# Taking the low part of the attention output through PSUM: one subtraction moved from VectorE to TensorE and ScalarE

## The chip, the cores and the metric

The kernel runs on one core of one Trainium2 chip. A core has five engines with a queue of instructions each: TensorE (PE in the tables, its weight loads PEld), VectorE (DVE), ScalarE (ACT), GpSimd (POOL) and SyncE (SP), which here only issues DMAs. The metric is the time of one execution in microseconds (us) on the device. The profile comes from one profiled execution of the same program.

## The reference

What is computed is a chain of three layers over a batch of 8 sequences of 576 positions with 512 features: attention in chunks of 64, a gated layer whose gate is a convolution over 5 positions, and a normalised two-matrix layer with a residual. Cut to its core:

```python
scores = np.matmul(q_c, k_c.transpose(0, 1, 2, 4, 3)) / np.sqrt(D)   # 64 x 64 in each chunk and head
scores = scores - np.max(scores, axis=-1, keepdims=True)
attn = np.exp(scores)
attn = attn / (np.sum(attn, axis=-1, keepdims=True) + 1e-09)
x = np.matmul(attn, v_c)                       # then heads are laid side by side: 512 features

for k in range(5):
    gate_pre += conv_w[k] * xp[:, k:k + S, :]  # xp is x with 4 zeros in front
gate = 1.0 / (1.0 + np.exp(-gate_pre))
x = gate * (x @ w_val) @ w_out

xn = (x - mu) / np.sqrt(var + 1e-06) * g_ln
out = x + np.maximum(xn @ w_ch1, 0.0) @ w_ch2  # 512 -> 2048 -> 512
```

Everything is float32. The large products are made with float32r operands, and each operand is split in a high part (its copy in float32r) and a low part (what the copy left), and a product is three matmuls: high by high, low by high, high by low.

## The kernel before

The 4608 positions are cut into 18 units of 256 and 9 blocks of 512 (two units make a block). In the first part of the program one slot follows another, one per unit. A slot issues, in this order: the scores of a unit (`a3`, tile `sc`, softmax on VectorE with tiles `mx`, `ex`, `sm`, `pr`), the turned weights of the unit before (`a4`, PSUM tile `pst`, copied by ScalarE to `pT`), and its product with the values (`a5`, PSUM tile `x`, two banks, one buffer). Between these stand the pieces of the gated layer for earlier blocks: the convolution (`conv`: one ScalarE instruction and four VectorE instructions for each of four slices of `cg`), its sigmoid (`sigm`, one ScalarE instruction over `cg`), the product with `w_val` (`val`: four chains of 12 matmuls into PSUM tile `psv`; `gv` multiplies by the gate on VectorE, `gh` and `gl` are its two parts) and the product with `w_out` (`proj`: four chains into `pso`, copied to `y` and stored). The chains of `psv` and `pso` share a pool of two PSUM buffers, so the third chain of `val` starts when `gv` has read the first.

After `a5` three copies of `x` are made: `xf` in float32, which the convolution reads, `xh`, the high part, and `xl`, the low part, which `val` reads a slot later. ScalarE makes `xf` (L233) and `xh` (L236), VectorE makes `xl` from `x` and `xh` (L238). Where a sequence begins inside a unit, `xf` has a gap of four columns there, and all three are made in two pieces (`segs`).

Weights come as 64-bit words and are decoded to float32 by one ScalarE and three VectorE instructions for each 128x512 tile (`decode`, tile `da`, L87 to L90). In the first part this is done for `w_val`, `w_out` and, by `early_ff`, for the first four pairs of tiles of the two last matrices.

From some 303 us on the second part (`ff1`, `ff2`, then `ff_pair`) does the last layer, almost all of it matmuls.

PE's order is as written in the code for the first four slots and in the second part. In the rest of the first part, and on the other engines, a scheduler places the instructions ahead of time, by its own estimates and by priorities; on the chip each engine then works strictly through its list.

Of the kernel before, what the change touches and what calls it, by code (L numbers as in the profile page):

```python
# [9 lines left out]
F32R = mybir.dt.float32r  # L10
U32 = mybir.dt.uint32
ACTF = mybir.ActivationFunctionType
ALU = mybir.AluOpType
# [6 lines left out]
def tile_chunk_attention_gated_mlp(ctx: ExitStack, tc: tile.TileContext, qk, v, w_val, conv_w, w_out, g_ln, w1, w2, out):  # L20
    nc = tc.nc
# [9 lines left out]
    P = 128  # L31
    BLK = 512
    UN = 256
    UPB = BLK // UN
    NB = NT // BLK
    NU = NT // UN
# [4 lines left out]
    LAG = 1  # L41
# [3 lines left out]
    scale = 1.0 / float(D) ** 0.5  # L45
    outf = out.rearrange("b s d -> (b s) d")

    def boundary(j):
        o = (-(j * BLK)) % S
        return o if 0 < o < BLK else BLK  # L50

    const = ctx.enter_context(tc.tile_pool(name="const", bufs=1))
# [18 lines left out]
    ident = const.tile([P, P], F32, name="ident")  # L71
    cw = const.tile([P, (KC + 1) * CT], F32, name="cw")
    gr = const.tile([CT, P], F32, name="gr")


    qkr, vr = {}, {}

    def load_qkv(u):
        t = qkr[u] = pA.tile([P, 2, NP, UN], F32, tag="qk", name="qkr")
        nc.sync.dma_start(out=t.rearrange("p a h t -> p (a h t)"), in_=qk[u])  # L80
        t = vr[u] = pA.tile([P, NC, NP, D], F32, tag="vr", name="vr", bufs=3)
        nc.sync.dma_start(out=t.rearrange("p c h d -> p (c h d)"), in_=v[u])
# [18 lines left out]
    def load_w(w, nm, slot0):  # L101
        raws = []
        for c in range(CT):
            raw = wA.tile([P, DM, 2], U32, tag=f"s{slot0 + c}", name="raw")
            nc.sync.dma_start(out=raw, in_=w[c * P:(c + 1) * P])
            raws.append(raw)
        wv[nm] = raws
# [73 lines left out]
    def a4(u):  # L181
        pr = pt.pop(u)
        t = pA.tile([P, NG, P], F32, tag="pT", name="pT", bufs=1)
        ps = ps_p.tile([P, NG, P], F32, tag="p", name="pst")
        for g in range(NG):
            nc.tensor.transpose(out=ps[:, g, :], in_=pr[:, g].rearrange("p r k -> p (r k)"), identity=ident)
        with tc.high_priority():
            nc.scalar.activation(out=t, in_=ps, func=ACTF.Copy)
            pT[u] = t

    xf, xh, xl = {}, {}, {}

    def new_block(j):
        o = boundary(j)
        t = pD2.tile([P, CT, BLK + 2 * HALO], F32, tag="xf", name="xf")
        if j == 0:
            nc.gpsimd.memset(t[:, :, 0:HALO], 0.0)
        else:
            ob = boundary(j - 1)
            e = BLK + (HALO if ob < BLK else 0)  # L200
            nc.gpsimd.tensor_copy(out=t[:, :, 0:HALO], in_=xf[j - 1][:, :, e:e + HALO])
        if o < BLK:
            nc.gpsimd.memset(t[:, :, HALO + o:2 * HALO + o], 0.0)
        xf[j] = t
        xh[j] = pD2.tile([P, CT, BLK], F32R, tag="xh", name="xh")
        xl[j] = pD2.tile([P, CT, BLK], F32R, tag="xl", name="xl")

    def a5(u):
        t = pT.pop(u)
        j, uu = divmod(u, UPB)  # L210
        va = vr.pop(u)
        x = ps_x.tile([P, 2, NP // 2, UN], F32, tag="x", name="x")
        for i in range(NP // 2):
            for c in range(NC):
                n, cs = c // 2, slice(c % 2 * CH, (c % 2 + 1) * CH)
                for f in range(2):
                    for r in range(2):
                        r0, o0 = CH * r, CH * f
                        nc.tensor.matmul(
                            out=x[o0:o0 + CH, r, i, c * CH:(c + 1) * CH],  # L220
                            lhsT=va[r0:r0 + CH, c, 2 * i + f, :],
                            rhs=t[r0:r0 + CH, n * NP + 2 * i + f, cs],
                            start=True, stop=True,
                        )
        if uu == 0:
            new_block(j)
        o = boundary(j)
        a, b = uu * UN, (uu + 1) * UN
        segs = [(max(a, lo), min(b, hi), sh) for lo, hi, sh in ((0, o, HALO), (o, BLK, 2 * HALO)) if max(a, lo) < min(b, hi)]
        with tc.high_priority():  # L230
            for lo, hi, sh in segs:
                dst = xf[j][:, :, lo + sh:hi + sh].rearrange("p (r i) t -> p r i t", r=2)
                nc.scalar.activation(out=dst, in_=x[:, :, :, lo - a:hi - a], func=ACTF.Copy)  # L233
            for lo, hi, sh in segs:
                dst = xh[j][:, :, lo:hi].rearrange("p (r i) t -> p r i t", r=2)
                nc.scalar.activation(out=dst, in_=x[:, :, :, lo - a:hi - a], func=ACTF.Copy)  # L236
                low = xl[j][:, :, lo:hi].rearrange("p (r i) t -> p r i t", r=2)
                nc.vector.tensor_tensor(out=low, in0=x[:, :, :, lo - a:hi - a], in1=dst, op=ALU.subtract)  # L238


    cg = pD1.tile([P, CT, BLK + HALO], F32, name="cg")
# [334 lines left out]


    make_identity(nc, ident)
    load_qkv(0)
    load_w(w_val, "v", 0)  # L580
    load_qkv(1)
# [4 lines left out]
    def warm(u, i):  # L586

        n = WARM.get((u, i), 0)
        if n:
            ps = ps_d.tile([P, BLK], F32, tag="d", name="psw")  # L590
            for _ in range(n):
                nc.tensor.matmul(out=ps[:, 0:P], lhsT=ident, rhs=ident, start=True, stop=True)

    def slot(u):
        d = [dense.get((u, i), []) for i in range(4)]
        if u + 2 < NU:
            load_qkv(u + 2)
        warm(u, 0)
        if u < NU:
            a3(u)  # L600
        warm(u, 1)
        for fn in d[0]:
            fn()
        if LAG <= u < NU + LAG:
            a4(u - LAG)
        warm(u, 2)
        for fn in d[1]:
            fn()
        if LAG <= u < NU + LAG:
            a5(u - LAG)  # L610
        warm(u, 3)
        for fn in d[2] + d[3]:
            fn()

    dense = {}
# [45 lines left out]
    for j in range(NB):  # L661
        u = UPB * (j + 1) + LAG - 1
# [20 lines left out]
    for u in range(NU + LAG + 4):  # L683
        if u == MANUAL:
            head.close()
        slot(u)
        if u == NU + LAG - 1:
            with tc.high_priority():
                sigm(NB - 1)
            prep()  # L690
# [58 lines left out]
    for s in range(NS):  # L749
        for p in range(NPR):  # L750
# [5 lines left out]
            if s + 1 < NS and 2 <= p < 6:  # L756
                i = 2 * (p - 2)
# [43 lines left out]
```

## Time and profile before

| | |
|---|---|
| median of 3 runs | 1139.91 us (1138.92 to 1139.91) |
| span of the profiled execution, first to last instruction | 1134.2 us |
| median less that span | 5.7 us |
| busy in the span: PE, weight loads | 1070.5 us (94%), 871.4 us (77%) |
| busy in the span: DVE, ACT, POOL | 712.8 us (63%), 483.5 us (43%), 110.6 us (10%) |

The page gives the span of the profiled execution, and no time of its own around it; the 5.7 us between its span and the median of the runs are taken as what lies before and after the instructions. Shares of the whole span mix the two parts: in the second part PE works almost without a pause, in the first it doesn't. The ends of matmuls are modelled, and one ends after the next has begun, so the distance between starts says what a matmul takes.

### The profile page before, as it was taken

Reading aid. Unit: us, or ns where it says so; the run is one execution under the profiler, and the core shown is the slowest. Engines: PE = TensorE matmul, PEld = TensorE weight load, DVE = VectorE, ACT = ScalarE, POOL = GpSimd, SP = SyncE. Lnnn points to the kernel's source line nnn. Section 1 sums busy time; section 2 is a strip of 40 time slices with the busy share of each in tenths; the row PEclk is TensorE's granted clock in tenths of the full one; section 3 lists DMA queues with packets and bytes.
Section 4 is the critical chain, followed back from the end, with each engine's and each line's share of the span. In section 5 each row is a group of like instructions: output and inputs, shape, how many; then the busy total and the mean of one; then the engine's idle time right before and its main releaser. Section 6 shows DMA issues by size and latency. Waiting matters only on the chain.

```text
span 1134.2 us, 17091 instructions
## 1 busy us (share of the span) xinstructions
PE 1070.5 (94%) x6862; PEld 871.4 (77%) x6862; DVE 712.8 (63%) x1171; ACT 483.5 (43%) x832; POOL 110.6 (10%) x120
## 2 busy tenths in 40 slices
PE   5788989899898989899999999999999999999998
PEld 5676767777786868688888888888888888878877
DVE  6999999888967877545647434447444437432434
ACT  3566666566574754434444123333223333221221
POOL 2021001000003443322210000000000000000000
PEclk9799999999999999999999999999999999999999
DMA  8535546531135753634342733332733222622212
GB/s 334 169 121 166 187 133 213 179 107 72 46 120 188 225 165 119 236 118 145 126 141 100 232 99 106 112 106 89 232 105 103 99 93 89 227 93 93 75 38 75
DMA packets 58581, 155.28 MB, mean 137 GB/s; under 512 B 5742, under 2 KB 13958, under 8 KB 56198
## 3 DMA queue, kind: packets, MB, share of 16 engines
q1 hardware_dynamic: 53318, 144.75, 37.7%
q10 hardware_dynamic: 5184, 9.44, 2.2%
q8 instruction: 54, 0.88, 0.3%
q14 instruction: 25, 0.20, 0.1%
HBM read 116.41 MB, written 37.75 MB: 136 GB/s over the span
## 4 chain that ended last, share of the span: by engine, by line
PE 65%; DVE 24%; issue 4%; ACT 3%; DMA 3%; POOL 0%; SPq 0%; ACTq 0%; POOLq 0%; DVEq 0%
PE acc L499 16%; PE x L525 15%; PE psf L499 14%; PE zy L525 10%; DVE cg L250 7%; PE psv L264 5%; DVE da L89 2%; DVE da L90 2%; DVE sm L176 2%; PE acc L385 1%; DVE xl L238 1%; DMA raw<-in_moe_w_ch 1%; DVE h L537 1%; PE psh L264 1%; DVE mx L167 1%
## 5 line engine op out<-in xcount | busy, mean ns | idle before, releaser
L545 DVE TENSOR_TENSOR c<-x,c 128x512 f32<-128x512 f32 x96 | 66.2, 690 | 237.3 <-ACT c L541 181.1
L499 PE MATMUL psf<-w,h 128*128 128x512 f32 x768 | 186.0, 391 | 0.0
L499 PE MATMUL acc<-w,h 128*128 128x512 f32 x768 | 186.0, 391 | 0.0
L499 PEld LDWEIGHTS acc<-w,h 128*128 128x128 f32 x768 | 144.2, 188 | 31.4
L499 PEld LDWEIGHTS psf<-w,h 128*128 128x128 f32 x768 | 144.2, 188 | 31.4
L525 PE MATMUL x<-t,wc 128*128 128x512 f32 x576 | 148.2, 393 | 3.4 <-DVE c L545 3.4
L541 ACT ACTIVATE c<-zy 128x512 f32<-128x512 f32 x96 | 58.0, 604 | 188.4 <-PE zy L525 188.3
L525 PEld LDWEIGHTS x<-t,wc 128*128 128x128 f32 x576 | 108.8, 189 | 27.8 <-DVE c L545 4.6
L536 ACT ACTIVATE h<-c 128x512 fp32r<-128x512 f32 x96 | 60.5, 631 | 136.1 <-DVE c L545 135.5
L250 DVE SCALAR_TENSOR_TENSOR cg<-xf,cw,cg 128x516 f32<-128x516 f32 (+1 forms) x176 | 108.6, 661 | 0.0
L504 DVE TENSOR_TENSOR yt<-psf,yt 128x512 f32<-128x512 f32 x128 | 88.2, 691 | 25.0 <-PE psf L499 21.1
L525 PE MATMUL zy<-b,wc 128*128 128x512 f32 x384 | 98.9, 393 | 0.0
L525 PEld LDWEIGHTS zy<-b,wc 128*128 128x128 f32 x384 | 71.2, 188 | 14.6
L537 DVE SCALAR_TENSOR_TENSOR h<-c,h 128x512 fp32r<-128x512 f32 x96 | 68.5, 713 | 14.0 <-ACT h L536 13.9
L264 PE MATMUL psv<-xh,vh 128*128 128x512 f32 x144 | 62.1, 432 | 15.5 <-DVE gv L282 15.5
L96 POOL TENSOR_TENSOR w<-da,w 128x512 fp32r<-128x512 f32 x32 | 48.6, 1526 | 128.8 <-ACT w L95 125.6
L264 PE MATMUL psv<-xh,vl 128*128 128x512 f32 x144 | 59.6, 414 | 0.0
L264 PE MATMUL psv<-xl,vh 128*128 128x512 f32 x144 | 59.6, 414 | 0.0
L264 PE MATMUL pso<-oh,gh 128*128 128x512 f32 x144 | 58.5, 406 | 0.1
L264 PE MATMUL pso<-oh,gl 128*128 128x512 f32 x144 | 56.5, 393 | 0.4 <-DVE gl L286 0.4
L264 PE MATMUL pso<-ol,gh 128*128 128x512 f32 x144 | 56.1, 390 | 0.0
L393 POOL TENSOR_TENSOR wc<-raws,wc 128x256 fp32r<-128x256 f32 x56 | 45.3, 831 | 107.4 <-ACT wc L392 100.5
(108 smaller groups left out, 1563.3 us busy)
## 6 DMA issues: line engine op xcount, KB each, us to landing
wc<-wc SPq DMA_DIRECT2D x112, 512.0 KB, 3.2
qkr<-in_qk SPq DMA_DIRECT2D x18, 1024.0 KB, 5.9
raw<-in_moe_w_ch SPq DMA_DIRECT2D x32, 512.0 KB, 4.2
vr<-in_v SPq DMA_DIRECT2D x18, 512.0 KB, 4.2
yd<-y ACTq DMA_DIRECT2D x36, 256.0 KB, 2.8
out<-yt SPq DMA_DIRECT2D x36, 256.0 KB, 3.7
yr<-yd SPq DMA_DIRECT2D x32, 256.0 KB, 3.2
yt<-yd SPq DMA_DIRECT2D x32, 256.0 KB, 4.1
```

The lines of the kernel that those rows point to most:

```text
L89: nc.vector.scalar_tensor_tensor(out=au, in0=hw, scalar=0x80000000, in1=au, op0=ALU.bitwise_and, op1=ALU.bitwise_or)
L96: nc.gpsimd.tensor_tensor(out=lo, in0=a, in1=hi, op=ALU.subtract)
L250: nc.vector.scalar_tensor_tensor(out=o, in0=x[:, f, i + lo:i + hi], scalar=cw[:, i * CT + f:i * CT + f + 1], in1=o, op0=ALU.mult, op1=ALU.add,
L264: nc.tensor.matmul(out=ps, lhsT=lt, rhs=rh, start=(i == 0), stop=(i == n - 1))
L393: eng.tensor_tensor(out=lo, in0=a, in1=hi, op=ALU.subtract)
L499: nc.tensor.matmul(out=ps, lhsT=lt, rhs=rh, start=(g == 0 and k == 0 and (first or half)), stop=(g == 1 and k == 2 and (last or half)),)
L504: nc.vector.tensor_tensor(out=yt[i], in0=ps, in1=yt[i], op=ALU.add)
L525: nc.tensor.matmul(out=ps, lhsT=lt, rhs=rh, start=(start and c == 0 and i == 0), stop=(c == 1 and i == 2), skip_group_check=True)
L536: nc.scalar.activation(out=t[:, 0, :], in_=src, func=ACTF.Relu)
L537: nc.vector.scalar_tensor_tensor(out=t[:, 1, :], in0=src, scalar=0.0, in1=t[:, 0, :], op0=ALU.max, op1=ALU.subtract)
L541: nc.scalar.activation(out=t, in_=zy, func=ACTF.Copy)
L545: nc.vector.tensor_tensor(out=t, in0=x, in1=t, op=ALU.add)
```

## The change

The subtraction on VectorE (L238) goes. In its place a new function `a6` adds minus the high part to `x` in PSUM: two matmuls (one for each bank of `x`) with the 128x128 matrix `minus`, which holds -1 on its diagonal. ScalarE then copies `x`, which now holds the low part, to `xl`. For that, the matmuls of `a5` no longer each start a new sum: only the first of them in each bank and row group does. The high part is now copied before `xf`, and `xh` and `xl` are made in one piece each. `a6` stands in the slot behind the work that follows `a5`. `minus` is made once at the start by ScalarE from the identity. The program's scratch for dynamic DMAs is set to 1024 bytes, so the tiles lie at other addresses.

```diff
+    minus = const.tile([P, P], F32R, name="minus")
...
-                            start=True, stop=True,
+                            start=(i == 0 and c == 0), stop=True, skip_group_check=True,
...
-            for lo, hi, sh in segs:
-                dst = xf[j][:, :, lo + sh:hi + sh].rearrange("p (r i) t -> p r i t", r=2)
-                nc.scalar.activation(out=dst, in_=x[:, :, :, lo - a:hi - a], func=ACTF.Copy)
-            for lo, hi, sh in segs:
-                dst = xh[j][:, :, lo:hi].rearrange("p (r i) t -> p r i t", r=2)
-                nc.scalar.activation(out=dst, in_=x[:, :, :, lo - a:hi - a], func=ACTF.Copy)
-                low = xl[j][:, :, lo:hi].rearrange("p (r i) t -> p r i t", r=2)
-                nc.vector.tensor_tensor(out=low, in0=x[:, :, :, lo - a:hi - a], in1=dst, op=ALU.subtract)
+            hi = xh[j][:, :, a:b].rearrange("p (r i) t -> p r i t", r=2)
+            nc.scalar.activation(out=hi, in_=x, func=ACTF.Copy)
+            for lo, up, sh in segs:
+                dst = xf[j][:, :, lo + sh:up + sh].rearrange("p (r i) t -> p r i t", r=2)
+                nc.scalar.activation(out=dst, in_=x[:, :, :, lo - a:up - a], func=ACTF.Copy)
+        rest[u] = x
+
+    def a6(u):
+        x = rest.pop(u)
+        j, uu = divmod(u, UPB)
+        a, b = uu * UN, (uu + 1) * UN
+        with tc.high_priority():
+            for r in range(2):
+                nc.tensor.matmul(
+                    out=x[:, r], lhsT=minus, rhs=xh[j][:, 2 * r:2 * r + 2, a:b],
+                    start=False, stop=True, skip_group_check=True,
+                )
+            nc.scalar.activation(out=xl[j][:, :, a:b].rearrange("p (r i) t -> p r i t", r=2), in_=x, func=ACTF.Copy)
...
+    nc.scalar.activation(out=minus, in_=ident, func=ACTF.Copy, scale=-1.0)
...
-        for fn in d[2] + d[3]:
+        for fn in d[2]:
+            fn()
+        if LAG <= u < NU + LAG:
+            a6(u - LAG)
+        for fn in d[3]:
             fn()
...
-    nc = bacc.Bacc("TRN2", target_bir_lowering=False, num_devices=1)
+    nc = bacc.Bacc("TRN2", target_bir_lowering=False, num_devices=1, dynamic_dma_scratch_size=1024)
```

The scheduler makes new lists for all engines. Three places of them follow; line numbers in the lists of after are larger (L222 was L219, L277 was L264, L263 was L250, L295 was L282, L89 to L91 were L88 to L90).

PE, behind the product of unit 10 (`x`); `psv` are the chains of `val`. Before:

```order
428 L264 MATMUL pso<-oh_793,gl 128x512
429 L219 MATMUL x<-pT,vr 64x64 x32
430 L264 MATMUL psv<-xh,vh_248 128x512
431 L264 MATMUL psv<-xl,vh_248 128x512
432 L264 MATMUL psv<-xh,vl_249 128x512
433 L264 MATMUL psv<-xh,vh_257 128x512
```

After:

```order
440 L222 MATMUL x<-pT,vr 64x64 x32
441 L277 MATMUL psv<-xh,vh_250 128x512
442 L277 MATMUL psv<-xl,vh_250 128x512
443 L277 MATMUL psv<-xh,vl_251 128x512
444 L277 MATMUL psv<-xh,vh_259 128x512
445 L277 MATMUL psv<-xl,vh_259 128x512
446 L277 MATMUL psv<-xh,vl_260 128x512
447 L277 MATMUL psv<-xh,vh_268 128x512
448 L277 MATMUL psv<-xl,vh_268 128x512
449 L277 MATMUL psv<-xh,vl_269 128x512
450 L247 MATMUL x<-xh,minus 128x512 x2
451 L277 MATMUL psv<-xh,vh_277 128x512
```

The two new matmuls stand nine matmuls behind `x`, inside the chains that follow it; so it is, with nine or ten, for every unit from 4 on, `pso` in place of `psv` for the odd ones.

DVE, ahead of the first `gv` of block 3 (the rows with 192 and 320 columns). Before:

```order
161 L250 SCALAR_TENSOR_TENSOR cg<-xf,cw,cg 128x516
162 L179 TENSOR_TENSOR pr<-ex_144,sm 128x1024
163 L250 SCALAR_TENSOR_TENSOR cg<-xf,cw,cg 128x516
164 L238 TENSOR_TENSOR xl<-x,xh 128x4x256
165 L88 TENSOR_SCALAR da<-da 128x512 x2
166 L89 SCALAR_TENSOR_TENSOR da<-raw_3474,da 128x512
167 L89 SCALAR_TENSOR_TENSOR da<-raw_3476,da 128x512
168 L90 SCALAR_TENSOR_TENSOR da<-raw_3474,da 128x512
169 L282 TENSOR_TENSOR gv<-psv,cg 128x192 x2
170 L282 TENSOR_TENSOR gv<-psv,cg 128x320 x2
```

After:

```order
162 L177 TENSOR_REDUCE sm<-ex_145 128x16
163 L263 SCALAR_TENSOR_TENSOR cg<-xf,cw,cg 128x516
164 L178 RECIPROCAL sm<-sm 128x16
165 L263 SCALAR_TENSOR_TENSOR cg<-xf,cw,cg 128x516
166 L180 TENSOR_TENSOR pr<-ex_145,sm 128x1024
167 L263 SCALAR_TENSOR_TENSOR cg<-xf,cw,cg 128x516 x4
168 L295 TENSOR_TENSOR gv<-psv,cg 128x192 x2
169 L295 TENSOR_TENSOR gv<-psv,cg 128x320 x2
```

The `xl` is gone, and so is the decoding ahead of this `gv`: all decoding of the first part now stands earlier in the list, some of it ahead of the gates of blocks 1 and 2. Up to this row the list of after has 12 `xl` fewer and 3 L88, 3 L89 and 4 L90 more; at the first `gv` of block 4 it has 14 `xl` fewer and the same decoding.

ACT, around the sigmoid of block 4 (`cg<-cg`), with the copies of units 10 and 11. Before:

```order
147 L233 ACTIVATE xf<-x 128x4x256
148 L236 ACTIVATE xh<-x 128x4x256
149 L257 ACT_TABLE_LOAD
150 L257 ACTIVATE cg<-cg 128x2064
151 L188 ACTIVATE pT<-pst 128x1024
152 L285 ACTIVATE gh<-gv 128x512 x2
153 L174 ACT_TABLE_LOAD
154 L174 ACTIVATE ex_143<-ex_143 128x16x64
155 L285 ACTIVATE gh<-gv 128x512 x2
156 L233 ACTIVATE xf<-x 128x4x64
```

After, the same stretch:

```order
164 L235 ACTIVATE xh<-x 128x4x256
165 L238 ACTIVATE xf<-x 128x4x256
166 L270 ACT_TABLE_LOAD
167 L270 ACTIVATE cg<-cg 128x2064
168 L251 ACTIVATE xl<-x 128x4x256
169 L298 ACTIVATE gh<-gv 128x512 x2
170 L175 ACT_TABLE_LOAD
171 L175 ACTIVATE ex_144<-ex_144 128x16x64
172 L189 ACTIVATE pT<-pst 128x1024
173 L298 ACTIVATE gh<-gv 128x512 x2
174 L235 ACTIVATE xh<-x 128x4x256
```

The new copy `xl` stands behind the sigmoid, where `pT` was; `pT` now stands behind the exponential.

## Rows read from the trace of the kernel before

**Rows 1.** Windows: three stretches; columns are named in the first line.

```profile
core 0: us, PE busy (x) PEld busy (x) DVE busy (x) ACT busy (x) POOL busy (x), PEclk, DMA share, GB/s
33.00:171.00 138.00, 116.46 (x1527) 94.73 (x1526) 130.62 (x199) 86.89 (x117) 17.47 (x19) 0.92 0.48 159
171.00:303.00 132.00, 121.21 (x1435) 97.88 (x1436) 117.27 (x176) 82.02 (x105) 5.45 (x8) 0.96 0.39 131
...
400.00:1134.00 734.00, 720.93 (x3168) 585.75 (x3166) 366.97 (x606) 242.68 (x478) 58.07 (x64) 1.00 0.36 124
```

**Rows 2.** Waits of PE, 33 to 333 us: total us, times, longest.

```profile
PE psv L264 <- DVE gv L282: 15.5, 6, 5.1
PE x L219 <- ACT pT L188: 11.7, 6, 3.2
```

**Rows 3.** Chain that ended last, 33 to 303 us, shares by line.

```profile
by line: DVE cg L250 29.9%; PE psv L264 14.7%; issue 7.7%; DVE sm L176 6.0%; DVE xl L238 5.3%; DVE pr L179 4.1%; DVE gv L282 3.9%; DVE mx L167 3.8%; ACT cg L257 3.6%; DVE ex L170 3.4%; DVE gl L286 2.6%; DMA raw<-in_moe_w_ch 2.5%; DVE da L89
```

**Rows 4.** Same chain, pieces around one release: start us, us, what.

```profile
268.18 1.94 ACT cg L257
270.12 0.02 issue
270.14 1.23 DVE gv L282 x3
271.37 0.14 issue
271.51 5.74 PE psv L264 x24
```

**Rows 5.** Groups by line, 0 to 333 us: count, busy us, mean ns.

```profile
L238 DVE TENSOR_TENSOR xl<-x,xh 128x1024 fp32r<-128x1024 f32 (+3 forms) x24 | 22.8, 950 | 1.9 <-ACT xh L236 1.9
```

**Rows 6.** Groups of the decoding on DVE, 33 to 171 us.

```profile
L89 DVE SCALAR_TENSOR_TENSOR da<-raw,da 128x512 uint32<-128x512 uint32 x11 | 7.4, 680 | 0.0
L90 DVE SCALAR_TENSOR_TENSOR da<-raw,da 128x512 uint32<-128x512 uint32 x10 | 6.8, 682 | 0.0
L88 DVE TENSOR_SCALAR da<-da 128x512 uint32<-128x512 uint32 x11 | 4.4, 410 | 0.0
```

**Rows 7.** Timeline of PE: releases of later `psv` pairs; start us, us, then [wait].

```profile
171.23 0.76 PE L264 MATMUL psv<-xh,vh 128*128 128x512 f32 x1 [5.09 <-DVE gv L282]
...
205.85 0.76 PE L264 MATMUL psv<-xh,vh 128*128 128x512 f32 x1 [2.98 <-DVE gv L282]
...
238.58 0.47 PE L264 MATMUL psv<-xh,vh 128*128 128x512 f32 x1 [2.22 <-DVE gv L282]
...
271.51 0.47 PE L264 MATMUL psv<-xh,vh 128*128 128x512 f32 x1 [2.28 <-DVE gv L282]
...
302.38 0.56 PE L219 MATMUL x<-pT,vr 64*64 64x64 f32 x18 [3.08 <-ACT pT L188]
302.88 0.49 PE L264 MATMUL psv<-xh,vh 128*128 128x512 f32 x1
```

**Rows 8.** Timeline of PE behind the release at 271.51 us.

```profile
283.93 1.16 PE L162 MATMUL sc<-qkr 64*64 64x64 f32 x64
...
298.26 1.04 PE L186 MATMUL pst<-ident,pr 128*128 128x128 f32 x8
```

**Rows 9.** Chain, 300 to 330 us: one unbroken run of `pso`.

```profile
309.44 11.11 PE pso L264 x48
```

**Rows 10.** Timeline of ACT: copies of units 13 and 14.

```profile
247.30 1.07 ACT L233 ACTIVATE xf<-x 128x512 f32<-128x512 f32 x2
248.25 0.60 ACT L236 ACTIVATE xh<-x 128x512 fp32r<-128x512 f32 x1
...
261.51 1.03 ACT L233 ACTIVATE xf<-x 128x1024 f32<-128x1024 f32 x1 [0.52 <-PE x L219]
262.43 1.02 ACT L236 ACTIVATE xh<-x 128x1024 fp32r<-128x1024 f32 x1
```

**Rows 11.** Timeline of PE behind unit 13: first and tenth `pso`.

```profile
246.95 0.50 PE L264 MATMUL pso<-oh,gh 128*128 128x512 f32 x1
...
249.13 0.39 PE L264 MATMUL pso<-oh,gh 128*128 128x512 f32 x1
```

**Rows 12.** Timeline of ACT at the start.

```profile
8.34 0.66 ACT L87 ACTIVATE da<-raw 128x512 f32<-128x512 f32 x1 [6.33 <-DMA raw<-in_moe_w_val]
```

More of the change, by code (lines that the diff above doesn't have):

```diff
@@ L206, in new_block @@
         xl[j] = pD2.tile([P, CT, BLK], F32R, tag="xl", name="xl")
+    rest = {}
     def a5(u):
```

## The prediction

> **What bounds the kernel now.** I read the windows first. From 400 us on PE is busy for 720.9 of 734 us: there only matmuls count, the change adds none, and what the first part gains or loses is handed on to the end. From 33 to 171 us DVE is busy for 130.6 of 138 us, PE for 116.5 at a mean clock of 0.92; from 171 to 303 us DVE for 117.3 of 132, PE for 121.2 at 0.96 [rows 1]. So the first part is DVE's as far as 171 us, and behind that it is shared. The waits of PE say how: between 33 and 333 us it stands still for 15.5 us until DVE has made `gv`, and for 11.7 us until ACT has made `pT` [rows 2]. The chain of waits says what is ahead of these: 29.9% is the convolution on DVE, 14.7% the `psv` chains, and 5.3% is `xl` itself [rows 3], 14 us of the 270 in that window. At one release it reads: the last convolution, the sigmoid 1.94 us, `gv`, and 3.3 us after the sigmoid began PE starts the second half of `psv` [rows 4]. That start comes once a block, and the distance between two such starts is the period.
>
> **What goes from DVE.** 24 instructions, 22.8 us [rows 5]. Not all of it falls off the path, for two reasons: the new list puts other work where `xl` was, and PE becomes the bound.
>
> *Up to the release at 171.23 us* (block 3). The list has 12 `xl` fewer there, 12 x 0.95 = 11.4 us, but decoding that stood behind this point now stands ahead of it: 3 L88, 3 L89 and 4 L90, 3 x 0.41 + 7 x 0.68 = 6.0 us [rows 5, 6]. The gain in DVE's work is 5.4 us. DVE is idle for only 7.4 us of this stretch, so the work bounds it, but a part of the gap was PE's or a DMA's. Bounds 0 and 5.4 us; I take the middle, 2.7.
>
> *From there to 302.9 us.* The releases stand at 171.23, 205.85, 238.58, 271.51 and 302.88 us: four periods, 131.65 us in all [rows 7]. In each PE waits 2.2 to 3.1 us before the next release [rows 7], so PE's own work is the floor. From 271.51 to the end of `pst` at 299.30 it works without a wait, 27.8 us; a `sc` of about 1.1 us, which this last period lacks, makes a full one 28.9 [rows 7, 8]. DVE's side: 117.3 us over four periods is 29.3 each [rows 1]. Two `xl` and more go (24 over 18 units, 2.5 us a block), and the decoding of this stretch has moved ahead: the two lists differ by 13.3 us of `xl` at the release of block 4, where the decoding is equal, against 5.4 at block 3, so 7.9 us go in the first of these periods alone. That leaves at most 26.8 us a period. To this comes the wait for the sigmoid, 1.96 us from the end of the convolution to `gv` [rows 4], so some 28.8. That is under PE's floor, by a margin of 1 to 2 us: here the bound changes hands.
>
> **What is added to PE.** Two matmuls of 512 columns for each unit. 48 such matmuls in an unbroken run take 11.11 us, 0.231 each [rows 9]; a pair is 0.46, a block 0.93. Between 0 (where the pair falls into a wait) and 0.78 us a pair (two durations of 0.39 as listed [rows 11]). Where PE is the bound I take 0.46.
>
> **The new wait.** The pair writes `x`, so PE can pass it only when both ACT copies, `xh` and `xf`, have read `x`. Behind it in PE's list stand the rest of the chain, `sc` and everything else. Behind unit 13 PE would reach the pair at the tenth `pso`, 249.13 us. ACT could start the first copy at 247.30, a whole copy takes 0.95 to the start of the next, the two pieces of `xf` 1.07: done at 249.3 [rows 10, 11]. A wait of 0.2 to 0.3 us. Behind unit 14 ACT stood waiting for `x` and ran both copies from 261.51 to 263.45, 1.94 us [rows 10]; PE comes nine matmuls, 2.1 us, after `x`: no wait. I take 0.35 us for a block.
>
> In the old kernel ACT waits for PE's writes of `x`, as the 0.52 us show [rows 10]; no PE write there meets a copy still reading. The Trainium skill (PSUM — Partial Sum Buffer, section "PSUM bank collisions raise a hardware error") says that two engines must not touch one bank in the same partitions at once, reads against writes too. By that rule the wait for `xf` stays whatever the order, as the sum has it; without the rule `xh` alone would count, the 0.35 would be nil, and the sum 1.4 us better over four periods. No run here tests it.
>
> **What is added to ACT.** 18 copies of 128x1024, 1.02 us as `xh` of that size [rows 10], 18 us; six small pieces of `xh` go. ACT is busy for 82 of 132 us [rows 1]; with 9 us more it has 41 left. In its list `xl` stands behind the sigmoid, just where ACT has to wait for `gv` anyway (1.23 us [rows 4]); that hides it, and if it did not, 1 us a block would come on top. `pT` moves behind the exponential. PE needs it only behind 24 matmuls and `pst`, 24 x 0.231 and 0.9, or 6.4 us after the release [rows 8, 9], so I count nothing. `minus` is made while ACT waits 6.33 us for the first weights [rows 12]: nothing. The smaller scratch changes addresses and lets four loads of `yt` go out earlier in the second part; I count nothing, within 2 us either way.
>
> **Sum.** New periods: 28.9 + 0.93 + 0.35 = 30.2 three times and 1.1 less for the last: 119.6 against 131.65, a gain of 12.0 us. With 2.7 from the stretch before, and 0.5 lost for unit 17's pair where PE has no wait any more: 14.2 us. The profiled span goes from 1134.2 to 1120.0 us. With the 5.7 us between that span and the median this is **1125.7 us**. Its own range: the early term 0 to 5.4, and the new waits from nothing to 1 us more a block: 1121 to 1133.
>
> **Rivals.**
>
> *All of it comes off.* If DVE bounds every block, before and after, all 22.8 us go: 1117.1 us. For it: DVE is the busier of the two as far as 171 us. Against it: PE's 28.9 us floor. The Trainium skill (Perfetto Trace Analysis, "Identifying the Most-Contended Engine") says to rank engines by occupancy, and TensorE by its weight loads rather than by its busy matmuls. By that rule DVE (117.3 of 132 us) stays ahead of PE (weight loads 97.9 of 132) after the change too, and this rival would come true. The starts in rows 8 and 9 speak against it: runs without a pause, while weight loads fill only part of them.
>
> *No change.* The gate moves from `gv` to `pT`. At 302.38 us PE already waits for it for 3.08 us [rows 7], 2.0 us on average [rows 2]. With `pT` later in ACT's list, 2 us in each of four periods give back 7.8, and pairs that don't hide in the five earlier blocks 4.7: gain 1.7, 1138.2 us. Against it: the sigmoid, from which all this starts, comes earlier too.
>
> *Slower.* The place is the pair on PE, the price ACT's delay. If one more ACT copy (1.03 us [rows 10]) stands ahead of the two in each unit, PE stands still 18 times: 18.5 us lost, 1144.2 us. It decides from 0.8 us for each unit on. For it: in the first blocks ACT also copies for the decoding, and waits for weights there. Against it: `x` stands just where ACT is idle and waits for PE (0.52 us [rows 10]), and early waits of PE absorb the same time.
>
> **Chances and range.** My forecast 0.72, all of it 0.12, no change 0.09, slower 0.07. About 0.2%, 2.3 us, is what a measurement tells from no change. The forecast's own range lies wholly below that, so faster 0.85, same 0.08, slower 0.07. The range for 8 in 10 reaches from the second case to beyond the own range: 1117 to 1135 us.
>
> **What would show it.** In the new profile: no L238 on DVE; releases of `psv` some 30 us apart from the fourth block on, with no wait for `gv` and a PE clock near 1 in that stretch; the pair at 0.46 us with waits under 0.5 us; the release of block 3 at 166 to 171 us; the second part as long as before. Wrong would be: periods that stay at 32 to 33 us, a wait for `pT` of 2 us in each block, or pairs that wait about 1 us for ACT.

## The result and the profile after

The changed kernel takes 1123.76 us in the median of 4 runs (1118.68 to 1124.99); the kernel before, run beside it, 1139.91. The ratio is 0.9857, 95% interval 0.983 to 0.9884: 16.3 us less, 13 to 19. The prediction was 1125.7 us. Its profiled run took 1124.91 us, its span is 1123.1 us, where the prediction had 1120.0.

The windows of the kernel after, to be laid beside [rows 1] (us, busy time and count of each engine, clock, DMA share):

```profile
33.00:171.00 138.00, 121.72 (x1546) 97.52 (x1546) 128.46 (x199) 97.53 (x129) 21.95 (x20) 0.94 0.56 185
171.00:303.00 132.00, 131.50 (x1542) 105.38 (x1541) 115.39 (x182) 94.38 (x119) 1.84 (x6) 1.00 0.31 112
```

Up to 171 us little has changed. From there to 303 us PE is busy for 131.5 of 132 us at the full clock, where it had been for 121.2 at 0.96. Its waits between 33 and 333 us (total us, times, longest) against [rows 2]:

```profile
PE psv L277 <- DVE gv L295: 4.5, 3, 2.4
PE pst L187 <- DVE pr L180: 4.0, 1, 4.0
PE x L222 <- ACT pT L189: 3.1, 3, 1.6
PE x L247 <- ACT xf L238: 2.2, 4, 1.2
PE sc L163 <- issue: 2.1, 1, 2.1
```

The wait for `gv` has gone from 15.5 to 4.5 us, that for `pT` from 11.7 to 3.1. The new wait of the pair (`x` L247) for `xf` comes four times in all. The releases of the later `psv`, in the timeline of PE, answer to [rows 7]:

```profile
170.45 0.47 PE L277 MATMUL psv<-xh,vh 128*128 128x512 f32 x1 [0.96 <-DVE gv L295]
...
200.84 0.50 PE L277 MATMUL psv<-xh,vh 128*128 128x512 f32 x1
...
230.80 0.50 PE L277 MATMUL psv<-xh,vh 128*128 128x512 f32 x1
...
260.77 0.50 PE L277 MATMUL psv<-xh,vh 128*128 128x512 f32 x1
...
289.82 0.48 PE L277 MATMUL psv<-xh,vh 128*128 128x512 f32 x1
```

Four periods of 30.39, 29.96, 29.97 and 29.05 us, 119.37 together against 131.65, and after the first of these releases none has a wait. Block 7 starts 13.06 us earlier than before (289.82 against 302.88), the span is 11.1 us shorter: some 2 us are lost again behind it. They are lost before the release of block 8, as the windows from the one release to the other show, first of the kernel before, then of the kernel after:

```profile
302.88:325.83 22.95, 22.95 (x144) 18.82 (x143) 21.00 (x57) 13.91 (x22) 0.00 (x0) 1.00 0.26 93
...
289.82:314.61 24.79, 24.55 (x171) 19.85 (x170) 21.69 (x58) 17.62 (x27) 0.00 (x0) 1.00 0.24 86
```

PE (the first busy time) has 27 matmuls more there. They belong to the last unit, and stood ahead of block 7's release before: 8 of `pst` and 17 of the 64 of `x`; the other two are the pair, with a wait of 0.24 us. From block 8's release to the end both kernels take the same, 808.4 and 808.5 us.

A part of the difference stands in no row of the prediction. Below are the first 5.8 us behind each of the four releases, in windows, of the kernel before:

```profile
171.23:177.03 5.80, 5.80 (x22) 4.76 (x23) 4.90 (x8) 2.52 (x5) 2.55 (x2) 0.68 0.92 332
205.85:211.65 5.80, 5.80 (x19) 4.64 (x20) 4.41 (x7) 3.88 (x5) 0.00 (x0) 0.73 0.94 336
238.58:244.38 5.80, 5.80 (x18) 4.59 (x19) 4.34 (x7) 3.90 (x5) 0.00 (x0) 0.71 0.16 68
271.51:277.31 5.80, 5.80 (x32) 4.54 (x36) 4.21 (x8) 3.90 (x5) 0.00 (x0) 1.00 0.00 0
```

and of two of them in the kernel after:

```profile
200.84:206.64 5.80, 5.80 (x36) 4.88 (x31) 5.27 (x8) 3.90 (x6) 0.00 (x0) 1.00 0.54 182
230.80:236.60 5.80, 5.80 (x36) 4.88 (x31) 5.20 (x7) 3.93 (x5) 0.00 (x0) 1.00 0.53 181
```

Behind three of the four old releases, each after a wait of 2.2 to 5.1 us, PE ran at a mean clock of 0.68 to 0.73, and behind the fourth at 1.00, after a wait of the same length. The cost can be read from PE's busy time in a whole period: 30.64 us from 238.58 to 271.51, where the run with whole pieces below has 28.86 for the same work at the full clock. That is 1.8 us for this release, in which PE did not wait but worked slowly. Most of it seems to reach the period, because DVE's last `gv` waits for the slow chains. DVE's timeline of the kernel before, behind the slow release at 238.58 and behind the one at the full clock:

```profile
245.97 0.76 DVE L282 TENSOR_TENSOR gv<-psv,cg 128x320 f32<-128x320 f32 x2 [2.13 <-PE psv L264]
...
277.27 0.76 DVE L282 TENSOR_TENSOR gv<-psv,cg 128x384 f32<-128x384 f32 x2 [1.59 <-PE psv L264]
```

The first `gv` of these blocks start at 237.29 and 270.14, so the last come 8.68 and 7.13 us behind them, 1.55 us apart. The two periods are 32.93 and 31.37 us, 1.56 apart, with the same work on DVE (27.86 and 27.76 us); the second has one `sc` less on PE.

### The profile page after: what moved, and what is told of

Its sections match the earlier page's. It is cut to its first block, busy times and chain, and to the rows that moved or that the text cites. A ratio compares the mean times of both kernels' runs of the same rounds, so it can differ in the third digit from the quotient of the medians.

```text
span 1123.1 us, 17137 instructions
## 1 busy us (share of the span) xinstructions
PE 1075.7 (96%) x6898; PEld 873.5 (78%) x6898; DVE 696.5 (62%) x1147; ACT 500.0 (45%) x845; POOL 112.0 (10%) x120
## 4 chain that ended last, share of the span: by engine, by line
PE 75%; DVE 14%; ACT 4%; issue 3%; DMA 2%; POOL 0%; SPq 0%; POOLq 0%; ACTq 0%; DVEq 0%
PE acc L512 16%; PE x L538 15%; PE psf L512 15%; PE zy L538 10%; PE psv L277 7%; PE pso L277 6%; DVE cg L263 2%; DVE da L91 2%; DVE da L90 2%; PE acc L398 1%; PE x L222 1%; DVE h L550 1%; PE psh L277 1%; PE pst L187 1%; PE pst L361 1%
## 5 line engine op out<-in xcount | busy, mean ns | idle before, releaser
L512 PEld LDWEIGHTS psf<-w,h 128*128 128x128 f32 x768 | 144.2, 188 | 31.4
L263 DVE SCALAR_TENSOR_TENSOR cg<-xf,cw,cg 128x516 f32<-128x516 f32 (+1 forms) x176 | 109.1, 667 | 4.0 <-ACT cg L261 3.6
L277 PE MATMUL psv<-xh,vh 128*128 128x512 f32 x144 | 59.7, 415 | 4.5 <-DVE gv L295 4.5
L277 PE MATMUL pso<-oh,gh 128*128 128x512 f32 x144 | 59.2, 411 | 0.1
L277 PE MATMUL psv<-xl,vh 128*128 128x512 f32 x144 | 57.7, 401 | 0.0
L277 PE MATMUL pso<-oh,gl 128*128 128x512 f32 x144 | 57.0, 396 | 0.6 <-DVE gl L299 0.6
L277 PE MATMUL psv<-xh,vl 128*128 128x512 f32 x144 | 57.3, 398 | 0.0
L277 PE MATMUL pso<-ol,gh 128*128 128x512 f32 x144 | 56.8, 394 | 0.0
```

Source lines behind the costliest of these rows:

```text
L263: nc.vector.scalar_tensor_tensor(out=o, in0=x[:, f, i + lo:i + hi], scalar=cw[:, i * CT + f:i * CT + f + 1], in1=o, op0=ALU.mult, op1=ALU.add,
L277: nc.tensor.matmul(out=ps, lhsT=lt, rhs=rh, start=(i == 0), stop=(i == n - 1))
L512: nc.tensor.matmul(out=ps, lhsT=lt, rhs=rh, start=(g == 0 and k == 0 and (first or half)), stop=(g == 1 and k == 2 and (last or half)),)
```

## The experiments

Times are medians; each ratio is to the kernel before, run on the same chip beside it. "Periods" are the distances between the releases of blocks 4, 5, 6 and 7.

| kernel | us | ratio, 95% interval | periods, us |
|---|---|---|---|
| before | 1137.85 to 1139.91 | 1 | 32.7, 32.9, 31.4 |
| after | 1123.76 | 0.9857 [0.983, 0.9884] | 30.0, 30.0, 29.1 |
| scratch alone | 1134.5 | 0.9967 [0.9953, 0.998] | 32.8, 32.9, 31.7 |
| subtraction twice | 1152.55 | 1.0136 [1.0119, 1.0153] | 33.8, 34.7, 34.4 |
| pair twice | 1124.35 | 0.9881 [0.9864, 0.9898] | 30.9, 30.9, 29.7 |
| no pair | 1127.85 | 0.9918 [0.9903, 0.9932] | 31.0, 30.8, 31.1 |
| copy by DVE | 1135.0 | 0.9971 [0.996, 0.9983] | 31.0, 31.1, 31.2 |
| small pair | 1126.26 | 0.989 [0.9872, 0.9909] | 29.8, 30.6, 30.1 |
| subtraction on GpSimd | 1155.94 | 1.0158 [1.0137, 1.0179] | 33.1, 34.3, 34.8 |
| whole pieces | 1129.82 | 0.993 [0.9908, 0.9952] | 30.8, 30.9, 30.9 |
| order only | 1132.54 | 0.9942 [0.9927, 0.9957] | 30.6, 32.1, 31.6 |
| pieces only | 1131.4 | 0.9932 [0.9914, 0.9949] | 30.8, 30.9, 31.0 |
| whole pieces, scratch | 1129.93 | 0.9912 [0.9893, 0.993] | 30.9, 30.9, 31.0 |
| mixed | 1125.27 | 0.9877 [0.986, 0.9894] | 30.2, 32.2, 30.1 |

**Scratch alone.** The kernel before with

```diff
+ dynamic_dma_scratch_size=1024
```

> The kernel before with the smaller scratch alone (all tiles at other addresses, four yt loads allowed earlier). Theory (the gain is VectorE's time in the first part, up to PE's floor): within 3 us of before, 1137 to 1142. Rival (a good part of the 16 us comes from addresses and earlier loads in the second part): 1125 to 1134.

1134.5 us, between the two, 3.8 us less by the ratio: "within 2 us either way" was too narrow. The first part is as before, release for release:

```profile
271.06 0.47 PE L264 MATMUL psv<-xh,vh 128*128 128x512 f32 x1 [2.29 <-DVE gv L282]
```

Its profiled span, 1133.1 us, is only 1.1 us shorter than that of before. So the gain is in the executions' times and the profile doesn't say where.

**The subtraction twice.** Before, with each `xl` written twice:

```diff
+ nc.vector.tensor_tensor(out=low, in0=x[...], in1=dst, op=ALU.subtract)
```

> The kernel before with each VectorE subtraction of the low part done twice (same result), 24 instructions and 22.8 us more of VectorE. Theory (VectorE sets the period before): nearly all of it shows, 1155 to 1165. Rival (the gain came from somewhere else, VectorE has slack): under 1146.

1152.55 us, 15.5 us slower, for 22.8 us more on DVE: short of the theory's range, and far from the rival's. DVE was the bound before, but not all the time: a third of the added work falls into its idle time. The windows (DVE is the third busy time) show 267.97 of 282 us:

```profile
33.00:171.00 138.00, 118.67 (x1529) 96.84 (x1529) 134.35 (x198) 82.00 (x112) 16.11 (x16) 0.92 0.47 155
171.00:315.00 144.00, 126.88 (x1480) 103.07 (x1478) 133.62 (x195) 84.98 (x108) 5.32 (x10) 0.92 0.37 124
```

**The pair twice.** After, with two matmuls of zeros besides:

```diff
- for r in range(2):
+ for m, r in ((minus, 0), (minus, 1), (zero, 0), (zero, 1)):
```

> The kernel after with two more matmuls for each unit that add zero times the high part to x (a zero matrix in place of minus identity; same result). Theory (PE sets the period after, some 30 us a block from block 3 on): 0.93 us more in each of the last four or five periods and at unit 17, up to as much in earlier blocks, 1128 to 1132, periods of 30.9 us. Rival (VectorE still sets it): unchanged within 2 us, 1122 to 1126, periods of 30.0.

The periods are what the theory said, 30.85 to 30.93, which is 0.93 more than 30.0 for two pairs: a pair costs 0.46 us wherever PE has no wait. PE's releases:

```profile
199.97 0.50 PE L278 MATMUL psv<-xh,vh 128*128 128x512 f32 x1
...
230.90 0.50 PE L278 MATMUL psv<-xh,vh 128*128 128x512 f32 x1
...
261.81 0.50 PE L278 MATMUL psv<-xh,vh 128*128 128x512 f32 x1
```

The median, 1124.35 us, is in the rival's range, the ratio 2.7 us above the changed kernel's: the two intervals overlap. The traces carry this (this run's span, 1127.2 us, is 4.1 us longer than the changed kernel's), not the median.

**No pair.** After, without the two matmuls; `xl` then holds a copy of `x`:

```diff
-   nc.tensor.matmul(out=x[:, r], lhsT=minus, rhs=xh[j][...], ...)
```

> The kernel after without the two matmuls: xl becomes a plain copy of x, so the low part is left out of what is computed, all else stays. Theory (PE's floor is 28.9 us without the pair): periods of 29 us, 4 to 6 us less than after, 1118 to 1120. Rival (VectorE sets the period after): unchanged, 1122 to 1125.

A miss on both sides: 1127.85 us, slower than with the pair. Without a wait for PE, ACT's third copy is placed straight behind the other two, ahead of the first tap of the convolution. ACT's timeline:

```profile
242.47 1.01 ACT L235 ACTIVATE xh<-x 128x1024 fp32r<-128x1024 f32 x1
243.38 1.08 ACT L238 ACTIVATE xf<-x 128x512 f32<-128x512 f32 x2
244.33 1.04 ACT L246 ACTIVATE xl<-x 128x1024 fp32r<-128x1024 f32 x1
245.24 0.62 ACT L307 ACTIVATE y<-pso 128x512 f32<-128x512 f32 x1
245.71 0.76 ACT L256 ACTIVATE cg<-xf,cw 128x516 f32<-128x516 f32 x1
```

DVE's own taps come behind it, and PE waits 1.65 to 1.74 us for `gv` again. So 1 us on ACT at that place lengthens the period by about as much, and the margin of the loop through DVE and ACT is below that.

**The copy by DVE.** After, with the third copy on VectorE:

```diff
- nc.scalar.activation(out=xl[j]..., in_=x, func=ACTF.Copy)
+ nc.vector.tensor_copy(out=xl[j]..., in_=x)
```

> The changed kernel, with one thing put back: after the pair of matmuls the low part is copied out of PSUM by VectorE (18 copies of 128x1024) instead of ScalarE; pair, whole pieces and scratch as changed. My theory: what counts is that VectorE is rid of the work, so nearly all of the gain that is not the scratch's goes: VectorE has some 18 x 1.0 us again, in place of 22.8, and PE the pair besides. 1133 to 1140 us, PE waiting for gv at the releases of blocks 3 to 7 again, periods of 32 us or more. Rival (the gain came from whole pieces and from xh ahead of xf on ScalarE): 1125 to 1129 us, as changed.

1135.0 us, as the theory said; PE waits for `gv` again. But the periods are 31.0 to 31.2, not 32 and more. Most of what is lost against the changed kernel is lost early: the release of block 3 is at 178.01 us, in place of 170.45. 18 such copies take DVE about as long as the subtraction did:

```profile
L251 DVE CAST xl<-x 128x1024 fp32r<-128x1024 f32 x18 | 21.9, 1217 | 2.6 <-PE x L247 2.6
```

**A small pair.** After, with an eighth of the pair's columns, to keep its wait and drop its work:

```diff
- out=x[:, r], lhsT=minus, rhs=xh[j][:, 2 * r:2 * r + 2, a:b],
+ out=x[:, r, :, 0:16], lhsT=minus, rhs=xh[j][:, 2 * r:2 * r + 2, a:a + 16],
```

> The changed kernel with the two matmuls of each unit cut to 16 of their 256 columns a chunk (64 columns in place of 512; the low part is then wrong in the rest), so that ScalarE's copy of the low part still waits for PE and stands nearly where it stands in the changed kernel. It puts the price of the pair apart from the order that the kernel without a pair changed with it. My theory: PE is the bound from block 3 on, so the periods fall from 30.0 to 29.1-29.4 us (two pairs a block, each 0.46 less 0.1), the whole to 1119 to 1122 us. Rival (VectorE and ScalarE are a loop of 30 us by themselves, PE's 30.0 is chance): periods stay at 29.9 to 30.9, 1123 to 1128 us.

1126.26 us, the rival's range; of the periods, 29.51, 29.76, 30.56 and 30.06 us, the first two lie between the two ranges and the others in the rival's. PE waits for `gv` again at the later ones:

```profile
203.23 0.50 PE L277 MATMUL psv<-xh,vh 128*128 128x512 f32 x1
...
232.99 0.47 PE L277 MATMUL psv<-xh,vh 128*128 128x512 f32 x1 [0.21 <-DVE gv L295]
...
263.55 0.47 PE L277 MATMUL psv<-xh,vh 128*128 128x512 f32 x1 [0.81 <-DVE gv L295]
...
293.61 0.47 PE L277 MATMUL psv<-xh,vh 128*128 128x512 f32 x1 [0.57 <-DVE gv L295]
```

The list has changed here too. In the changed kernel DVE's `pr`, 1.22 us, stands behind the last tap in the full periods that follow the release of block 4, and lies in the wait for the sigmoid. Here it has 0, 1, 2 and 1 taps behind it, in the order of the four periods, and the periods go with that number. DVE's timeline at the third:

```profile
257.40 1.22 DVE L180 TENSOR_TENSOR pr<-ex,sm 128x1024 f32<-128x1024 f32 x1
258.54 1.54 DVE L263 SCALAR_TENSOR_TENSOR cg<-xf,cw,cg 128x516 f32<-128x516 f32 x2
262.19 1.42 DVE L295 TENSOR_TENSOR gv<-psv,cg 128x384 f32<-128x384 f32 x4 [2.11 <-ACT cg L270]
```

Where `pr` has no tap behind it, PE is nearly the bound and the period is 29.5, half a us under the changed kernel's. So the pair's price is real, and a list that suits less takes it back.

**The subtraction on GpSimd.** Before, with the small scratch and

```diff
- nc.vector.tensor_tensor(out=low, in0=x[...], in1=dst, op=ALU.subtract)
+ nc.gpsimd.tensor_tensor(out=low, in0=xf[j][...], in1=dst, op=ALU.subtract)
```

> The kernel before with the smaller scratch, and the subtraction on GpSimd, which reads the copy in SBUF instead of PSUM (24 pieces; 128x512 take 1.33 to 1.53 us there, so some 3 us for a unit): VectorE is rid of it, PE has no pair, ScalarE no third copy. My theory: the place that does it doesn't matter as long as it is not VectorE, and PE's floor of 28.9 us a block is lower without the pair: periods of 29 to 29.9 us, 1117 to 1121 us, faster than the changed kernel. Rival (GpSimd is late: psv waits for xl, or VectorE is slower while GpSimd works): periods of 31 us and more, 1125 to 1135 us.

1155.94 us, slower than before by 18 us, worse than the rival's range. `xl` is not what is late: DVE is slower while GpSimd works. GpSimd's timeline, and DVE's of the same time:

```profile
267.15 3.53 POOL L238 TENSOR_TENSOR xl<-xf,xh 128x512 fp32r<-128x512 f32 x2
282.89 2.39 POOL L238 TENSOR_TENSOR xl<-xf,xh 128x1024 fp32r<-128x1024 f32 x1 [12.21 <-ACT xh L236]
```

```profile
267.15 2.37 DVE L179 TENSOR_TENSOR pr<-ex,sm 128x1024 f32<-128x1024 f32 x1
...
283.23 2.60 DVE L250 SCALAR_TENSOR_TENSOR cg<-xf,cw,cg 128x516 f32<-128x516 f32 x1
```

The same `pr` takes 1.22 us elsewhere, the same tap 0.74. Over 33 to 333 us a tap of 516 takes 0.92 us in the mean, against 0.76 before. The Trainium skill (SBUF — State Buffer, section "SBUF: two separate sides") says that a DVE operation with two SBUF inputs and a GpSimd operation that reads SBUF exclude each other for the whole instruction. These rows are in accord with that: DVE loses 1.2 and 1.9 us while GpSimd runs for 3.5 and 2.4.

**Whole pieces.** Before, with the order and pieces of the change on ACT, and the subtraction on DVE in one piece:

```diff
+ nc.scalar.activation(out=hi, in_=x, func=ACTF.Copy)
  (xf, piece by piece)
+ nc.vector.tensor_tensor(out=low, in0=x, in1=hi, op=ALU.subtract)
```

> The kernel before with ScalarE's high part ahead of the full copy and in one piece for each unit, and the subtraction still on VectorE but in one piece (18 instructions instead of 24); scratch as before, no pair. My theory: this part of the change is worth only the short instructions saved, 18 x 1.08 in place of 22.8 us on VectorE, some 2 to 4 us: 1134 to 1137 us. Rival (order on ScalarE carries much of the gain): 1130 us or less.

1129.82 us: 8.0 us less by the ratio, the rival's range, with nothing moved to PE. The periods are 30.8 to 30.9 us. DVE is busy for 27.84 us in one, as long as before (27.85), so no work has gone there. Whole periods in windows, of this kernel (third busy time is DVE):

```profile
234.49:265.36 30.87, 28.86 (x368) 23.47 (x369) 27.84 (x42) 19.43 (x25) 0.88 (x1) 1.00 0.36 133
```

and of the kernel before:

```profile
238.58:271.51 32.93, 30.64 (x369) 24.63 (x369) 27.86 (x43) 19.67 (x26) 0.70 (x1) 0.95 0.31 109
```

Two things have changed. PE's clock doesn't fall behind the release (28.86 us busy in place of 30.64). And `xl` stands elsewhere in DVE's list. The end of the convolution in DVE's timeline, of the kernel before:

```profile
266.27 1.22 DVE L238 TENSOR_TENSOR xl<-x,xh 128x1024 fp32r<-128x1024 f32 x1
267.40 0.74 DVE L250 SCALAR_TENSOR_TENSOR cg<-xf,cw,cg 128x516 f32<-128x516 f32 x1
270.14 1.42 DVE L282 TENSOR_TENSOR gv<-psv,cg 128x384 f32<-128x384 f32 x4 [2.00 <-ACT cg L257]
```

and with whole pieces:

```profile
261.26 0.75 DVE L249 SCALAR_TENSOR_TENSOR cg<-xf,cw,cg 128x516 f32<-128x516 f32 x1
261.93 1.22 DVE L237 TENSOR_TENSOR xl<-x,xh 128x1024 fp32r<-128x1024 f32 x1
264.00 1.42 DVE L281 TENSOR_TENSOR gv<-psv,cg 128x384 f32<-128x384 f32 x4 [0.85 <-ACT cg L256]
```

Before, the subtraction delays the last tap, and with it the sigmoid, for which DVE then stands idle 2.00 us. With whole pieces it lies in that idle time, of which 0.85 us are left.

The 2.1 us between these two periods are both things together, and the trace hints that the clock is the larger: in the period from block 6 to block 7 the clock is full in both kernels, and there 31.37 us stand against 30.93. In the traces of the three kernels with whole pieces no period from block 4 on has a slow stretch; whether the place of `xl` does that is not shown. Nor does every execution go so: three of the six of this kernel had a mean clock of 0.971 to 0.976 and took 1130.35 to 1132.81 us, the others, with the profiled one, 0.982 to 0.985 and 1128.16 to 1129.3 us.

**Order only.** Before, with all pieces of `xh` ahead of `xf` on ACT, 24 pieces as before:

```diff
+ (xh, piece by piece)
  (xf, piece by piece)
+ (xl, piece by piece)
```

> The kernel before with one thing changed: ScalarE makes the high part ahead of the full copy; 24 pieces, subtraction on VectorE and scratch as before. In VectorE's list xl still stands ahead of the last tap of the convolution. My theory (the 9 us of the run with whole pieces came from where xl stands on VectorE: behind the last tap, in the time in which VectorE waits for the sigmoid, and not among the taps): about half of it is missing here, periods of 31.8 to 32.5 us, 1133 to 1137 us. Rival (what counts is that ScalarE makes the high part first): periods of 30.9 us, 1128 to 1131 us.

1132.54 us, between the ranges and nearer to the theory's. One period has `xl` behind the last tap (DVE idles 0.86 us for the sigmoid) and takes 30.64, at a mean clock of 0.94; the next two have it ahead (1.99 us idle) and take 32.08, this one at the full clock, and 31.62. Of the 1.44 us between the first two, 1.14 are work on DVE (26.76 and 27.90 us): one `mx` (1.2 us) stands on the other side of the release. So the 1.1 us of idle time are shown, and what they are worth in a period is not.

**Pieces only.** Whole pieces, but with ACT making `xf` first, as before:

```diff
  (xf, piece by piece)
+ nc.scalar.activation(out=hi, in_=x, func=ACTF.Copy)
+ nc.vector.tensor_tensor(out=low, in0=x, in1=hi, op=ALU.subtract)
```

> The kernel before with the high part and the subtraction in one piece for each unit (18 of each in place of 24), ScalarE's order as before (full copy first), scratch as before. In VectorE's list xl stands behind the last tap, as in the run with whole pieces. My theory (place on VectorE): as that run, periods of 30.8 to 31.0 us, 1128.5 to 1131.5 us. Rival (ScalarE's order): periods of 32 us and more, 1134 to 1138 us.

1131.4 us and periods of 30.84, 30.91 and 30.96: the theory. ACT's order is not what counts.

**Whole pieces with the small scratch.**

```diff
+ dynamic_dma_scratch_size=1024
```

> The run with whole pieces, with the smaller scratch of the change besides: all of the change but the work on TensorE and the third copy on ScalarE. My theory: the parts add up, 1129.8 less 3.8 is 1126 us (1125 to 1127.5), so that the move from VectorE to TensorE and ScalarE itself is worth the 2 to 3 us that are left to the changed kernel. Rival (the scratch's gain overlaps with that of the pieces): 1129 to 1131 us, the move is worth 5 us or more.

1129.93 us, ratio 0.9912: the rival. On top of whole pieces the scratch gives 0.0018 of the ratio, less than the intervals can tell from nothing. This is all of the change but PE's pair and ACT's copy. The changed kernel's ratio is 0.0055 lower, 6 us, between 2.5 and 10 by the two intervals (taken on different chips). Part of that may be PE's clock: two of the six executions here had 0.983 and took 1125.02 and 1127.72 us, the other four 0.973 to 0.974 and 1129.63 to 1130.39, while those of the changed kernel had 0.983 to 0.986. In the traces it reaches block 7 5.9 us earlier (289.82 against 295.73), and its span is 2.8 us shorter.

**Mixed.** After, but the first unit of each block is subtracted by DVE in one piece, without a pair:

```diff
+ if uu == 0:
+     nc.vector.tensor_tensor(out=low, in0=x, in1=hi, op=ALU.subtract)
+     return
```

> The changed kernel, but for the first unit of each block VectorE subtracts in one piece (9 of 128x1024, without a pair on TensorE and a third copy on ScalarE); VectorE's list has these mostly behind the last tap, where it waits for the sigmoid. My theory: they are hidden there, PE's floor falls by one pair to 29.5 us a block, and the loop of VectorE and ScalarE stays under that: periods of 29.5 to 29.8 us, 1120 to 1123 us. Rival (that loop takes 30.0 us whatever PE does, as the run with the small pair showed, and the decoding falls behind early): periods of 30.0 to 30.9 us, 1123.5 to 1128 us.

1125.27 us, in the rival's range: no better than the changed kernel. Where `xl` stands behind the last tap the periods are 30.15 and 30.12 us, and DVE idles for 0.86 and 0.36 us before `gv`. In one block the list has it ahead of the last tap: 1.99 us idle, a period of 32.17. Of these 2 us the place in the list explains 1.1, the longer wait for the sigmoid; DVE also waits 2.00 us for ACT's first tap in that block, against 1.15 in the one before. None of the kernels run here beats the changed one.

## Why the prediction was right, step by step

**The sum.** A gain of 14.2 us was predicted on the span, 11.1 came in the profiled run and 16.3 by the ratio. The 5.7 us around the span were mis-sized: they mixed two executions of before (its span and a median), while in the runs here 1.7 to 2.1 us lie around the span of the same execution. With 1.8 us the forecast would have been 1121.8; the span came 3.1 us longer than forecast. These two errors offset each other, so that 1125.7 lies within 2 us of the median is in part luck. The profiled execution of before was one of its quicker ones: on record they take from 1135.05 us, at a mean granted clock of 0.980, to 1141.62, at 0.971, and the profiled one had 0.977. With 1.8 us around its span it took some 1136 us, 3.9 below the median, and this is most of what the ratio's gain is larger by than that of the two spans.

**Up to block 3.** 2.7 us predicted, 0.8 came (171.23 to 170.45), inside the bounds: DVE's work is 2.2 us less up to 171 us, where the prediction had counted 5.4, and its idle time grew. The decoding that moved ahead costs 8.1 us more in this stretch and not 6.0, and one more `mx` falls into it, 1.2 us.

**The four periods.** 119.6 us predicted, 119.37 came. The terms behind it: the floor of 28.9 us is shown by the run with whole pieces (28.86 busy), the pair's 0.46 by the run with two pairs (0.93 for two). The wait for `xf`, put at 0.35 a block, came only once in these four, 0.26 us (elsewhere 0.24, 0.48 and 1.20). That it comes at all says nothing on the rule on PSUM that the prediction weighed: the pair overwrites the values that `xf` is copied from, so it has to wait for that copy with or without the rule, and the prediction's other case, in which `xh` alone counts, could not have come. The floor was read from the one period of before at the full clock. So the sum held the clock's rise without naming it: PE is busy 1.7 to 1.8 us less by it in each of the two middle periods, and some 1.6 us of the period are that, by the comparison above.

**"Here the bound changes hands", by 1 to 2 us.** The bound does change hands, but this step is mis-sized: the margin is half a us. In the changed kernel the timelines of DVE and ACT have, ahead of the release of block 5,

```profile
211.67 6.09 DVE L263 SCALAR_TENSOR_TENSOR cg<-xf,cw,cg 128x516 f32<-128x516 f32 x9 [1.07 <-ACT cg L261]
...
226.87 1.93 ACT L270 ACTIVATE cg<-cg 128x2064 f32<-128x2064 f32 x1
...
228.83 0.76 DVE L295 TENSOR_TENSOR gv<-psv,cg 128x320 f32<-128x320 f32 x2 [1.74 <-ACT cg L270]
```

Four `gv` take 1.42 us where nothing holds them up, so they could be done at 230.25; PE begins at 230.80. The prediction added to DVE's work only the sigmoid, 1.96 us from the end of the convolution to `gv`. Here these are 2.9 us (225.96 to 228.83), with `pr` in them, because ACT comes to the sigmoid 0.9 us after the last tap, behind its copies of `x` and a table load. DVE also waits 1.07 us for ACT's first tap, and 0.5 for `ex`. The kernels with no pair and with the small pair showed how thin this is: 1 us on ACT, or `pr` ahead of two taps, and DVE and ACT are the bound again at 30.6 to 31 us.

**"What goes from DVE".** The 22.8 us went, and they matter (doubling them costs 15.5). But that they had to go elsewhere is not shown: with `xl` in one piece, DVE keeping all of it, 8.0 of the 16.3 us come as well, in part, it seems, by PE's clock. The prediction priced the pieces of ACT and DVE, a few short instructions, at next to nothing, and took the list to lose `xl` where it stood; it did not ask what `xl` cost at its place, ahead of the last tap. Moving the work to PE and ACT adds about 6 us to that (2.5 to 10), and the scratch 3.8 us alone but at most a little on top. These parts overlap, and how much of each is the place of `xl`, the clock or the list at large is not separated.

**ACT.** 18 copies of 1.02 us are hidden, as said: 18.3 us.

```profile
256.86 1.93 ACT L270 ACTIVATE cg<-cg 128x2064 f32<-128x2064 f32 x1
258.69 1.00 ACT L251 ACTIVATE xl<-x 128x1024 fp32r<-128x1024 f32 x1
```

They are hidden by their place, here behind the sigmoid. The run without a pair shows the price elsewhere, about 1 us a block, as the prediction had it.

**The rivals.** "All of it" did not come: PE is busy for 131.5 of 132 us. By the rule of the Trainium skill on ranking engines (Perfetto Trace Analysis, "Identifying the Most-Contended Engine"), which judges TensorE by MFU (its share of the peak rate, not worked out here) and weight loads, DVE, 115.4 us, still leads weight loads, 105.4, and would still be the bound; PE's unbroken work, and the 0.9 us a period that two more pairs cost, contradict it, and the loop through DVE and ACT, half a us shorter, is idle time in good part, which no ranking by busy time shows. "No change" fell with the waits for `pT`, 3.1 us in all. "Slower" would have needed 0.8 us in each unit at the pair; the waits for `xf` are 2.2 us over 18 units.

## What to carry to other kernels

Before work is moved off a busy engine, look at where it stands in that engine's list: ahead of the last link before another engine's step, a subtraction of 1.22 us made DVE wait 1.1 us longer here than behind that link. A loop through two engines has as its length their work plus every wait between them, not only the longest one. And where PE is released after a wait, read the granted clock of the next microseconds, since the price of the wait may go on there.

## What the runs showed of the hardware

PE's granted clock was 0.68 to 0.73 in the mean over the 5.8 us behind some releases, between its two levels of 1.2 and 2.4 GHz (matmuls of 512 columns start 0.43 us apart in the slow stretches and 0.23 in the others), and not behind others after waits of the same length: 2.22 us before the one at 238.58, 2.28 before that at 271.51, in one trace. What decides it is left open.

A DVE operation on two SBUF tensors took up to 2.60 us in place of 0.74 while GpSimd subtracted from SBUF; GpSimd needed 2.64 us in the mean for 128x1024.

DVE copies 128x1024 out of PSUM in 1.22 us, as long as it needs to subtract there.
